# Retention and a PReLU MLP on one core: the order of all engines written out by hand

## The chip, the cores and the metric

The kernel runs on one core of a Trainium2 chip. The metric is device time in microseconds (us) of one execution, taken as the median of several; less is better. A core has TensorE (PE, whose weight loads are a row of their own, PEld), VectorE (DVE), ScalarE (ACT), GpSimd (POOL) and SyncE (SP), which here issues nearly all DMAs. Each engine works through its own instructions in order and waits on semaphores for the others.

## The reference

```python
scores = scale * np.matmul(q, k.transpose(0, 1, 3, 2))        # (8, 8, 576, 64)
gamma = 1.0 - 2.0 ** (-5.0 - np.arange(H))
Dmat = np.where(rel >= 0, gamma[:, None, None] ** rel, 0.0)    # rel = i - j
attn = np.matmul(scores * Dmat, v)
x = attn.transpose(0, 2, 1, 3).reshape(4608, 512)
h = x @ w_in                                                    # 512 -> 2048
g = np.maximum(h, 0.0) + alpha * np.minimum(h, 0.0)
out = g @ w_out                                                 # 2048 -> 512
```

Eight batches of eight heads go through a retention (attention without softmax, with a decay for each head); its result, 4608 tokens of 512, goes through two matrix products with a PReLU between them. All of it is float32.

## The kernel before

**The MLP.** Tokens come in 18 blocks `kb` of 256 (`TB`), the hidden width in eight units `u` of 256. A *cell* is one block with one unit; there are 144. PE works on rounded operands (`float32r`), so each float32 operand is split into an upper part, the exact rest and a correction, three tiles in all: ACT makes the upper part, DVE the correction, POOL the rest (`split`, L317 to 321). A cell has 24 matmuls for the first product (`mm_h`, L350, line L358) into two PSUM banks, one for each half f of the unit, tags `psh0` and `psh1`; each holds two sums of 256 columns, `ph[:, 0]` and `ph[:, 1]`. `post_h` (L364) joins the two sums of each half (ACT copy L369, DVE L370), takes the PReLU of both halves together (ACT Relu of the negative at L372 and of the positive at L373, 512 columns each, then one DVE operation for each half at L376) and splits the result into `g`. The second product (`mm_o`, L385, line L396) has 12 matmuls into four banks `po`. After the last unit of a *visit* (a block's stay with two or four units), `evacuate` (L403) joins those sums, adds what an earlier visit stored (L412) and stores `o` to DRAM (L414).

**Order of visits.** `order` (L417) first runs units 0 to 3 for all blocks and then 4 to 7; blocks 14 to 17 come in short visits in between, while the weights of units 4 to 7 are taken in. A piece of weights costs ACT L287, L288 and L311, DVE L295 to L298 and L312, POOL L300 and L314 (`piece_in`, `piece_mid`, `piece_lim`). `prepare` (L335) fetches a block's x (from the tile `xb` that the attention filled, which it also stores to DRAM, or later back from DRAM) and splits it into `lx`.

**The attention.** Batch 0 is done by the `part_` functions at the start. The other 28 pairs (a batch, two heads) are done one at a time: loads of `kx`, `qx`, `kn`, `vn` by twelve DMAs (`load_pair`, L118), scaling of q on POOL and k on ACT (`scale_pair`, L441), transposes to `kT` and `qT` on DVE (L455), and then `joint(n)` (L544). It writes pair n-1's values (`pair_values`, 32 + 4 small matmuls L526, into two banks of the tags `psh0` and `psh1`, the same as ph's), the last chunk's scores (L552), pair n's scores (L491) and chunk states (L497); starts the DMA `mt<-qT` (L501); makes the masked scores `mt` (DVE L505, ACT L512, POOL L514) and copies the values into `xb` (L536). Running sums `su` of the states (L466 to L474) go by DMA into `vn` (L480), where the next joint's values read them. `kx`, `qx`, `mt`, `kT` and `qT` have one buffer each.

**What sets the order.** The setup, batch 0 and cells 0 to 3 stand under `tc.manual_schedule()`: each engine runs them as written. `ordered.close()` and a barrier end that. In the loop over cells 4 to 143 the text only gives priorities, and the tile framework's scheduler orders each engine's instructions. On PE it keeps cells' first products going and then sets two second products behind one another, just ahead of a joint's values. `todo` says which cell has a joint after it, `later` is a list of attention work put off to the next cells, `late` says which cells take in late weights.

Of the kernel before, what the change touches and what calls it, by code (L numbers as in the profile page):

```python
# [21 lines left out]
def kernel(  # L22
# [95 lines left out]
    def load_pair(n):  # L118
        b, c = pairs[n]
        kx, qx, kn = [nat.tile([P, S], FP32, tag=t, name=f"{t[0:2]}_{n}")  # L120
                      for t in ("kx", "qx", f"kn{n % 2}")]
        kx, qx = [t.rearrange("p (n r) -> p n r", r=32) for t in (kx, qx)]
        kn = kn.rearrange("p (j d) -> p j d", d=D)
        vn = vns[n % 2]
        load_sq(kx, k, b, c)
        load_sq(qx, q, b, c)
        for t, src in ((vn, v), (kn, k)):
            for h2 in range(2):
                load_head(t[half(1 - h2), h2] if t is vn else t[half(1 - h2)], src, b, 2 * c + h2)
        return kn, kx, qx, vn  # L130
# [186 lines left out]
    def split(to, w):  # L317
        nc.scalar.mul(piece(to[0]), w, BELOW)  # L318
        nc.vector.scalar_tensor_tensor(out=piece(to[2]), in0=to[0], scalar=ONE, in1=w,  # L319
                                       op0=ALU.mult, op1=ALU.subtract)  # L320
        nc.gpsimd.tensor_tensor(out=piece(to[1]), in0=w, in1=to[0], op=ALU.subtract)  # L321
# [9 lines left out]
    xb, ready_x = {}, {}  # L331
# [3 lines left out]
    def prepare(vis):  # L335
        kb = vis["kb"]
        if vis.get("x") is not None:
            return
        if kb in xb:
            x = xb.pop(kb)  # L340
            nc.sync.dma_start(x_kept[kb], x.rearrange("p c t -> p (c t)"))
        else:
            x = ring.tile([P, NCC, TB], FP32, tag=f"x{taken[0] % 2}", name=f"xr_{taken[0]}")
            taken[0] += 1
            nc.sync.dma_start(x.rearrange("p c t -> p (c t)"), x_kept[kb])
        to = lpool.tile([P, 3, NCC, TB], FP32, tag="lx", name=f"lx_{vis['n']}")
        vis["x"] = [to[:, l] for l in range(3)]
        split(vis["x"], x)
# [14 lines left out]

    def post_h(cell):  # L364
        u = cell["u"]
        gb, gc = [mlp.tile([P, 2, TB], FP32, tag=t, name=f"{t}_{cell['n']}") for t in ("gb", "gc")]
        for f in range(2):
            ph = cell["ph"][f]
            nc.scalar.copy(gc[:, f], ph[:, 1])  # L369
            nc.vector.scalar_tensor_tensor(out=gb[:, f], in0=ph[:, 0], scalar=ONE,  # L370
                                           in1=gc[:, f], op0=ALU.mult, op1=ALU.subtract)
        nc.scalar.activation(gc, gb, ACTF.Relu, scale=-1.0)  # L372
        nc.scalar.activation(gb, gb, ACTF.Relu)  # L373
        for f in range(2):
            fc = 2 * u + f
            nc.vector.scalar_tensor_tensor(out=gb[:, f], in0=gc[:, f],  # L376
                                           scalar=nalpha[:, fc:fc + 1], in1=gb[:, f],
                                           op0=ALU.mult, op1=ALU.add)
        g = mlp.tile([P, 3, 2, TB], FP32, tag="g", name=f"g_{cell['n']}")
        cell["g"] = g  # L380
        split([g[:, l] for l in range(3)], gb)
# [3 lines left out]
    def mm_o(cell):  # L385
# [14 lines left out]
        if cell["last"]:  # L400
            evacuate(vis)

    def evacuate(vis):  # L403
        kb = vis["kb"]
        for m in range(2):
            t = mlp.tile([P, DM], FP32, tag="gc", name=f"t{m}_{vis['n']}")
            o = ring.tile([P, DM], FP32, tag=f"o{m}", name=f"o{m}_{vis['n']}")
            nc.scalar.copy(t, acc[2 * m + 1])  # L408
            nc.vector.scalar_tensor_tensor(out=o, in0=acc[2 * m], scalar=ONE, in1=t,  # L409
                                           op0=ALU.mult, op1=ALU.subtract)  # L410
            if vis["has"]:
                nc.gpsimd.tensor_tensor(out=o, in0=o, in1=vis["o"][:, m], op=ALU.add)  # L412
            t0 = kb * TB + m * P
            nc.sync.dma_start(out[t0:t0 + P, :] if vis["final"] else o_kept[kb][:, m], o)  # L414
# [9 lines left out]
    for n, (kb, us) in enumerate(order):  # L424
        vis = {"kb": kb, "n": n, "has": seen[kb] > 0}
        seen[kb] += len(us)
        vis["final"] = seen[kb] == NU
        visits.append(vis)
        for u in us:
            cells.append({"vis": vis, "u": u, "first": u == us[0], "last": u == us[-1],  # L430
                          "n": len(cells)})
# [9 lines left out]
    def scale_pair(n):  # L441
        c = pairs[n][1]
        kn, qx = loaded[n][0], loaded[n][2]
        qh = qx.rearrange("p (j x) r -> p j x r", x=2)
        nc.gpsimd.tensor_tensor(out=qh, in0=qh,
                                in1=tabx[:, None, c, :, None].to_broadcast([P, NJ, 2, 32]),
                                op=ALU.mult)
        knf = kn.rearrange("p j d -> p (j d)")
        nc.scalar.activation(knf, knf, ACTF.Copy, scale=tabk[:, c:c + 1])

    def transposes(n):
        kT = attn.tile([P, S], FP32, tag="kT", name=f"kT_{n}")
        qT = attn.tile([P, S], FP32, tag="qT", name=f"qT_{n}")
        for src, dst in ((loaded[n][1], kT), (loaded[n][2], qT)):
            nc.vector.transpose(dst, src.rearrange("p n r -> p (n r)"))  # L455
        return kT, qT
# [4 lines left out]
    def running_sums(n, even, odd):  # L461
# [5 lines left out]
        for h2 in range(2):  # L467
            nc.vector.scalar_tensor_tensor(  # L468
                out=su[half(h2), 1::2], in0=su[half(h2), 0::2], scalar=g1[half(h2)],
                in1=odd[half(1 - h2)], op0=ALU.mult, op1=ALU.add)  # L470
        for j in range(3, NJ - 1, 2):
# [4 lines left out]
        return su  # L476
# [5 lines left out]
    def pair_front(n, kT, qT, kn, vn, extra):  # L482
        c = pairs[n][1]
        mts[n] = mt = attn.tile([P, 2 * S], FP32, tag="at", name=f"mt_{n}").rearrange(
            "p (h j s) -> p h j s", h=2, s=C)
        assert C == D and NJ == 9
        ps = [ps_tile([P, 2, NM - 1, C], f"ps{p2}_{n}") for p2 in range(2)]
        for j in range(NJ - 1):
            for h2 in range(2):
# [3 lines left out]
                                 start=True, stop=True, skip_group_check=True)  # L493
        for j in range(NJ - 1):
            for h2 in range(2):
# [3 lines left out]
                                 skip_group_check=True)  # L499
        for h2 in range(2):  # L500
            nc.sync.dma_start(mt[half(h2), h2].rearrange("p j s -> p (j s)"), qT[half(h2)])  # L501
# [6 lines left out]
        for h2 in range(2):  # L508
# [8 lines left out]
        later.append(lambda: pair_sums(vn, running_sums(n, ps[0][:, 1], ps[1][:, 1])))  # L517
# [22 lines left out]
    def operands(n):  # L540
        scale_pair(n)
        turned[n] = transposes(n)

    def joint(n):  # L544
        pv = [ps_h.tile([P, 8, C], FP32, tag=f"psh{m}", name=f"pv{m}_{n}") for m in range(2)]
        extra = pv[1][:, 7]

        def last_chunk():
            if n < len(pairs):
                kT, qT = turned[n]  # L550
                for h2 in range(2):
                    nc.tensor.matmul(extra[half(1 - h2)], kT[half(h2), chunk(NJ - 1)],  # L552
                                     qT[half(h2), chunk(NJ - 1)], start=True, stop=True)

        if n - 1 in mts:
# [3 lines left out]
        if n == len(pairs):  # L559
            return  # L560
        pair_front(n, *turned.pop(n), loaded[n][0], loaded[n][3], extra)
        if n + 1 < len(pairs):
            if n + 1 not in loaded:
                loaded[n + 1] = load_pair(n + 1)
            later.append(lambda: operands(n + 1))
# [155 lines left out]
    def now(n):  # L721
        prepare(cells[n]["vis"])
        mm_h(cells[n])
# [29 lines left out]
    now(0)  # L753
# [18 lines left out]
    now(1)  # L772
# [7 lines left out]
    now(2)  # L780
# [4 lines left out]
    loaded[NPAIR] = load_pair(NPAIR)  # L785
    piece_mid(2)
    now(3)
# [8 lines left out]
    loaded[NPAIR + 1] = load_pair(NPAIR + 1)  # L796
    ordered.close()
    tc.no_sync_barrier()
# [6 lines left out]
    for b in range(2, B):  # L805
        n = NS * sum(ready[kb] == b - 1 for kb in range(2, 13)) or 6
        for i, x in enumerate({8: (0, 2, 3, 5), 12: (1, 4, 6, 9), 6: (0, 1, 3, 4)}[n]):
# [10 lines left out]
    for key in ((17, 3), (16, 2), (16, 3), (15, 2), (15, 3), (14, 2), (14, 5), (15, 4), (15, 5),  # L818
                (16, 4), (16, 5), (17, 4), (17, 5)):
        work(base[key], 2 if key in ((17, 3), (15, 3), (15, 4)) else 1)  # L820
    assert sum(late.values()) == len(pieces) // 2

    done = set()
    for cell in cells[4:]:
        n = cell["n"]
        prepare(cell["vis"])
        mm_h(cell)
        post_h(cell)
        pend.append(cell)
        if len(pend) > 2:  # L830
            mm_o(pend.pop(0))
# [4 lines left out]
        if later:  # L836
            later.pop(0)()
        for x in todo.get(n, ()):
            while later:
                later.pop(0)()  # L840
            joint(x)
            done.add(x)
        if cell["vis"]["n"] + 1 < len(visits):
            follows = visits[cell["vis"]["n"] + 1]
            kb = follows["kb"]
            if kb not in xb or NPAIR * (ready[kb] + 1) in done:
                prepare(follows)
# [6 lines left out]
        piece_lim(late.get(n, 0))  # L854
    while pend:
        mm_o(pend.pop(0))
# [28 lines left out]
```

## Time and profile before

| | |
|---|---|
| median of 3 runs (lowest to highest) | 1221.22 us (1218.66 to 1222.59) |
| the profiled execution's own time | 1220.45 us |
| its span, first to last instruction | 1218.7 us |
| PE busy | 1014.9 us, 83% |
| DVE busy | 786.8 us, 65% |
| POOL busy | 670.2 us, 55% |
| ACT busy | 608.1 us, 50% |
| mean granted TensorE clock | 0.92 |
| HBM read, written | 78.52 MB, 31.46 MB |

Busy time counts the instructions' own durations; registers, branches, semaphores and DMA issue are not in it. A row of instructions is named by its line, engine, operation and tiles (out<-in, buffer numbers left out). An arrow in a wait (`A <- B`) means that A's engine sat idle until B ended. `SPq` rows are SP issuing DMAs. The granted clock is the share of its full speed that PE was given.

### The profile page before, as it was taken

The page shows a single profiled execution, that of the slowest core. Times are in us where ns is not written, and L with a number is a line of the kernel's source. Part 1 is how long each engine was busy: PE and PEld are TensorE (multiplying, and loading weights), DVE is VectorE, ACT ScalarE, POOL GpSimd, SP SyncE. Part 2 cuts the span into 40 slices and gives each one's busy share as a digit, 9 for nine tenths or more (in the row PEclk, how much of TensorE's full clock was granted, in tenths as well). Part 3 has the DMA queues.
Part 4 walks back from the last instruction along what each step waited for, and adds up shares of the span by engine and source line. Part 5 has one row for each costly group of instructions (what it writes and reads, how often), then busy time and mean ns, then how long its engine had stood idle before and what let it go on. Part 6 is the DMA issues. An engine that isn't in the chain of part 4 may idle for free.

```text
span 1218.7 us, 22971 instructions
## 1 busy us (share of the span) xinstructions
PE 1014.9 (83%) x8813; PEld 873.0 (72%) x8813; DVE 786.8 (65%) x1306; ACT 608.1 (50%) x1219; POOL 670.2 (55%) x414
## 2 busy tenths in 40 slices
PE   5672757789788987887888876869999999999998
PEld 4562546667577766776667765758889999999996
DVE  7666646375575665473655889896776666666664
ACT  4544335455454545453555646535554555555553
POOL 6766425354354453453535667776765565665554
PEclk8775777899898999998999999989999999999999
DMA  9244366454533535554554323413232122122111
GB/s 238 89 115 121 75 133 143 103 129 112 116 107 76 133 93 136 112 139 90 124 136 158 118 92 117 138 36 123 93 131 69 62 79 70 61 79 70 48 57 52
DMA packets 250589, 127.08 MB, mean 104 GB/s; under 512 B 217952, under 2 KB 217968, under 8 KB 250480
## 3 DMA queue, kind: packets, MB, share of 16 engines
q1 hardware_dynamic: 248368, 125.08, 38.4%
q8 instruction: 69, 1.13, 0.4%
q10 hardware_dynamic: 2112, 0.53, 0.2%
q14 instruction: 40, 0.33, 0.1%
HBM read 78.52 MB, written 31.46 MB: 90 GB/s over the span
## 4 chain that ended last, share of the span: by engine, by line
PE 33%; DVE 12%; ACT 6%; issue 5%; POOL 4%; DMA 2%; SPq 0%; POOLq 0%; ACTq 0%; DVEq 0%
PE po L396 16%; PE ph L358 15%; DVE gb L376 4%; POOL g L321 2%; ACT mt L512 1%; DVE gb L370 1%; ACT g L318 1%; PE pv L526 1%; DVE o L409 1%; DVE w L312 1%; DVE wc L295 1%; DVE su L468 1%; ACT lx L318 1%; POOL wc L300 1%; ACT gb L373 1%
## 5 line engine op out<-in xcount | busy, mean ns | idle before, releaser
L396 PE MATMUL po<-w,g 128*128 128x512 f32 x1728 | 465.3, 417 | 73.7 <-POOL g L321 34.4
L358 PE MATMUL ph<-lx,w 128*128 128x256 f32 x3456 | 469.5, 293 | 59.4 <-DVE gb L370 38.2
L358 PEld LDWEIGHTS ph<-lx,w 128*128 128x128 f32 x3456 | 448.6, 199 | 83.2 <-DVE gb L370 49.1
L396 PEld LDWEIGHTS po<-w,g 128*128 128x128 f32 x1728 | 333.0, 200 | 164.5 <-POOL g L321 47.7
L321 POOL TENSOR_TENSOR g<-gb,g 128x512 fp32r<-128x512 f32 x144 | 250.3, 1738 | 267.5 <-ACT g L318 226.3
L376 DVE SCALAR_TENSOR_TENSOR gb<-gc,nalpha,gb 128x256 f32<-128x256 f32 x288 | 209.1, 766 | 78.6 <-ACT gb L373 77.6
L318 ACT ACTIVATE g<-gb 128x512 fp32r<-128x512 f32 x144 | 90.8, 631 | 198.4 <-DVE gb L376 151.5
L319 DVE SCALAR_TENSOR_TENSOR g<-g,gb 128x512 fp32r<-128x512 f32 x144 | 122.5, 851 | 68.2 <-ACT g L318 67.5
L372 ACT ACTIVATE gc<-gb 128x512 f32<-128x512 f32 x144 | 90.6, 629 | 93.0 <-DVE gb L370 93.0
L514 POOL TENSOR_TENSOR mt<-mt,mask 64x512 f32<-64x512 f32 x56 | 71.7, 1281 | 117.8 <-issue 111.2
L370 DVE SCALAR_TENSOR_TENSOR gb<-ph,gc 128x256 f32<-128x256 f32 x288 | 115.4, 417 | 28.1 <-ACT gc L369 17.7
L369 ACT COPY gc<-ph 128x256 f32<-128x256 f32 x288 | 102.4, 367 | 55.7 <-PE ph L358 53.9
L373 ACT ACTIVATE gb<-gb 128x512 f32<-128x512 f32 x144 | 91.0, 632 | 7.6
L321 POOL TENSOR_TENSOR lx<-xr,lx 128x1024 fp32r<-128x1024 f32 x24 | 80.3, 3348 | 12.8 <-ACT lx L318 12.8
L321 POOL TENSOR_TENSOR lx<-xb,lx 128x1024 fp32r<-128x1024 f32 x18 | 59.6, 3313 | 46.4 <-ACT lx L318 42.2
L536 ACT COPY xb<-pv 128x256 f32<-128x256 f32 (+3 forms) x84 | 24.0, 320 | 121.2 <-PE pv L526 108.7
L412 POOL TENSOR_TENSOR o<-o,op 128x512 f32<-128x512 f32 x48 | 65.8, 1372 | 27.1 <-DVE o L409 23.6
L526 PEld LDWEIGHTS pv<-mt,vn 128*64 128x64 f32 x1008 | 42.9, 149 | 46.6 <-DMA vn<-su 18.4
L526 PE MATMUL pv<-mt,vn 128*64 128x64 f32 x1008 | 52.5, 243 | 27.5 <-DMA vn<-su 16.7
L409 DVE SCALAR_TENSOR_TENSOR o<-po,t 128x512 f32<-128x512 f32 x84 | 57.3, 683 | 25.7 <-ACT t L408 25.4
L300 POOL TENSOR_TENSOR wc<-wc,raw 128x512 int32<-128x512 int32 x32 | 46.2, 1444 | 36.6 <-DVE wc L298 22.6
L468 DVE SCALAR_TENSOR_TENSOR su<-su,gch,ps 64x256 f32<-64x256 f32 x56 | 26.9, 480 | 55.3 <-ACT su L466 54.4
(108 smaller groups left out, 789.0 us busy)
## 6 DMA issues: line engine op xcount, KB each, us to landing
ok<-o SPq DMA_DIRECT2D x48, 256.0 KB, 2.7
xr<-xk SPq DMA_DIRECT2D x24, 512.0 KB, 3.3
op<-ok SPq DMA_DIRECT2D x24, 512.0 KB, 3.7
xk<-xb SPq DMA_DIRECT2D x18, 512.0 KB, 3.7
out_dram<-o SPq DMA_DIRECT2D x36, 256.0 KB, 2.1
raw<-in_moe_w_in_dram SPq DMA_DIRECT2D x32, 256.0 KB, 3.7
raw<-in_moe_w_out_dram SPq DMA_DIRECT2D x16, 512.0 KB, 3.4
kx<-in_k_dram SPq DMA_DIRECT2D x112, 72.0 KB, 2.6
```

The lines of the kernel that those rows point to most:

```text
L318: nc.scalar.mul(piece(to[0]), w, BELOW)
L319: nc.vector.scalar_tensor_tensor(out=piece(to[2]), in0=to[0], scalar=ONE, in1=w, op0=ALU.mult, op1=ALU.subtract)
L321: nc.gpsimd.tensor_tensor(out=piece(to[1]), in0=w, in1=to[0], op=ALU.subtract)
L358: nc.tensor.matmul(ph[:, b], piece(w_at[u, cc // 2][:, l, (cc % 2 * 2 + f) * P: (cc % 2 * 2 + f + 1) * P]), piece(x[l][:, cc]), start=(n = ...
L369: nc.scalar.copy(gc[:, f], ph[:, 1])
L370: nc.vector.scalar_tensor_tensor(out=gb[:, f], in0=ph[:, 0], scalar=ONE, in1=gc[:, f], op0=ALU.mult, op1=ALU.subtract)
L372: nc.scalar.activation(gc, gb, ACTF.Relu, scale=-1.0)
L373: nc.scalar.activation(gb, gb, ACTF.Relu)
L376: nc.vector.scalar_tensor_tensor(out=gb[:, f], in0=gc[:, f], scalar=nalpha[:, fc:fc + 1], in1=gb[:, f], op0=ALU.mult, op1=ALU.add)
L396: nc.tensor.matmul(acc[2 * m + b], piece(g[:, l, f, m * P:(m + 1) * P]), piece(w_at[u, 2 + f][:, l]), start=(cell["first"] and f == 0 and ...
L514: nc.gpsimd.tensor_tensor(out=mt[to, h2, 0:NJ - 1], in0=mt[to, h2, 0:NJ - 1], in1=mask[to, None, :].to_broadcast([C, NJ - 1, C]), op=ALU.mult)
L526: nc.tensor.matmul(pv[j >= j1][half(h2), j - (j1 if j >= j1 else 0)], vn[:, h2, j], mt[:, h2, j], start=True, stop=True)
```

## The change

- The manual schedule now goes on to the end of the kernel; the barrier is gone. Every engine runs what the loop over cells writes, in that order.
- `post_h` becomes stages, of one half of a cell where it can be: `sum_h(cell, f)`, `prelu(cell, f)`, `upper_g`, `lower_g`. The negative Relu is written back into `ph[:, 1]`, in PSUM, and DVE reads it there; half 1 of a cell followed by a joint (`short`) keeps it in SBUF. `upper_g` and `lower_g` of a cell run within the next cell.
- `mm_o` runs two cells behind `mm_h`, always between two cells' first products. `evacuate` is called for each half of a block, with other work between.
- The attention's pieces are put into `later` with a mark, "v" or "s", and popped at fixed places of a cell. A joint's scores stand ahead of the values, and its states behind the last chunk.
- `prepare` becomes `fetch_x` and `split_x` (two halves of 512 columns); `x_ahead` makes them for the next visit and fetches x back from DRAM for the visit after it.
- Loads of a pair: v, then q, k and `kn` (before: k, q, v, `kn`). Four joints of an 8-cell batch stand at cells 0, 2, 4, 6 (before 0, 2, 3, 5), of a 12-cell batch at 1, 4, 7, 10 (before 1, 4, 6, 9). Late weights come one piece a cell (before up to two).

```diff
-    def split(to, w):
+    def upper(to, w):
         nc.scalar.mul(piece(to[0]), w, BELOW)
+    def lower(to, w):
         nc.vector.scalar_tensor_tensor(out=piece(to[2]), in0=to[0], scalar=ONE, in1=w,
                                        op0=ALU.mult, op1=ALU.subtract)
         nc.gpsimd.tensor_tensor(out=piece(to[1]), in0=w, in1=to[0], op=ALU.subtract)
...
+    def sum_h(cell, f):
...
+        ph, t = cell["ph"][f], cell["t"]
+        nc.scalar.copy(t[:, f], ph[:, 1])
+        nc.vector.scalar_tensor_tensor(out=cell["g"][:, f], in0=ph[:, 0], scalar=ONE,
+                                       in1=t[:, f], op0=ALU.mult, op1=ALU.subtract)
+    def prelu(cell, f):
+        ph, g, fc = cell["ph"][f], cell["g"][:, f], 2 * cell["u"] + f
+        below = cell["t"][:, f] if f in cell.get("short", ()) else ph[:, 1]
+        nc.scalar.activation(below, g, ACTF.Relu, scale=-1.0)
+        nc.scalar.activation(g, g, ACTF.Relu)
+        nc.vector.scalar_tensor_tensor(out=g, in0=below, scalar=nalpha[:, fc:fc + 1],
+                                       in1=g, op0=ALU.mult, op1=ALU.add)
...
-        later.append(lambda: pair_sums(vn, running_sums(n, ps[0][:, 1], ps[1][:, 1])))
+        sums = running_sums(n, ps[0][:, 1], ps[1][:, 1])
+        next(sums)
+        later.append(("v", lambda: pair_sums(vn, next(sums))))
+        if n + 1 < len(pairs):
+            later.append(("v", lambda: scale_q(n + 1)))
+        later.append(("s", lambda: masked(0)))
+        later.append(("s", lambda: masked(1)))
...
+        if ps:
+            pair_scores(n, ps)
         if n - 1 in mts:
             pair_values(n - 1, loaded.pop(n - 1)[3], mts.pop(n - 1), pv, last_chunk)
...
+                load_v(n + 1)
+                load_kq(n + 1)
+            later.append(("v", lambda: transpose(n + 1, 0)))
+            later.append(("v", lambda: transpose(n + 1, 1)))
+            later.append(("s", lambda: scale_k(n + 1)))
...
-    ordered.close()
-    tc.no_sync_barrier()
...
+    def x_ahead(vis):
+        for x in visits[vis["n"] + 1:vis["n"] + 2]:
+            start_x(x)
+            if "from" in x:
+                split_x(x)
...
     for cell in cells[4:]:
...
         mm_h(cell)
-        post_h(cell)
+        before = cells[n - 1] if n > 4 else None
+        sum_h(cell, 0)
+        if before:
+            upper_g(before)
+            lower_g(before)
+        pop("v")
+        prelu(cell, 0)
+        x_ahead(vis)
+        if joints:
+            cell["short"] = (1,)
+        sum_h(cell, 1)
+        pop("v")
+        if stage_c:
+            piece_lim(1)
+        prelu(cell, 1)
         pend.append(cell)
+        second = None
         if len(pend) > 2:
-            mm_o(pend.pop(0))
+            second = pend.pop(0)
+            mm_o(second)
+            if second["last"]:
+                evacuate(second["vis"], 0)
+        x_ahead(vis)
+        pop("s")
+        if second and second["last"]:
+            evacuate(second["vis"], 1)
...
+        pop("s", 2)
+        for x in joints:
+            pop("vs", len(later))
             joint(x)
...
         piece_in(late.get(n, 0))
         piece_mid(late.get(n, 0))
-        piece_lim(late.get(n, 0))
...
+    ordered.close()
```

## The prediction

> **What bounds the kernel now.** I first cut the span into stages, by the view of busy time by stretch. Its columns are the stretch, its length, then busy us of PE, weight loads, DVE, ACT and POOL (counts in brackets), the granted PE clock, the DMA share and GB/s.
>
> ```profile
> 0.00:110.00 110.00, 60.41 (x937) 50.66 (x937) 73.42 (x133) 50.14 (x94) 69.71 (x66) 0.77 0.57 147
> 110.00:205.00 95.00, 60.16 (x685) 49.56 (x686) 55.87 (x91) 39.28 (x82) 45.34 (x29) 0.72 0.47 106
> 205.00:650.00 445.00, 375.44 (x3994) 309.89 (x3994) 253.35 (x490) 220.75 (x470) 202.68 (x126) 0.94 0.50 117
> 650.00:700.00 50.00, 40.95 (x273) 36.38 (x272) 36.86 (x55) 29.53 (x59) 29.05 (x15) 0.93 0.40 131
> 700.00:800.00 100.00, 74.33 (x414) 62.89 (x413) 90.79 (x115) 53.16 (x101) 71.24 (x42) 0.94 0.33 108
> 800.00:850.00 50.00, 42.42 (x227) 36.14 (x226) 39.72 (x55) 24.15 (x48) 36.44 (x22) 0.86 0.26 90
> 850.00:1218.00 368.00, 361.21 (x2295) 327.47 (x2293) 236.83 (x370) 191.08 (x370) 215.76 (x117) 1.00 0.22 73
> ```
>
> From 850 us on PE is busy all the time at full clock. From 700 to 800 DVE is (90.8 of 100). From 205 to 650 no engine is: PE has 70 us of holes and a clock of 0.94. Before 205 everything waits. So only the first 850 us can be won. What a cell costs when PE never waits, the chain in order of time shows, from anywhere in the last stage:
>
> ```profile
> 959.83 2.87 PE ph L358 x24
> 962.70 2.75 PE po L396 x12
> ```
>
> A cell (a block of 256 tokens with one `u`; 24 + 12 matmuls) is 5.62 us of PE. How many cells a stage holds, the ph matmuls by stretch say (busy us of PE, count in brackets):
>
> ```profile
> 205.00:650.00 445.00, 149.68 (x1130) 0.94 0.50 117
> 650.00:850.00 200.00, 86.04 (x598) 0.91 0.33 109
> ```
>
> 1130/24 = 47.1 cells in the attention stage, 9.4 us each, and 598/24 = 25 in the late-weights stage, 8.0 us each, where 5.62 would do. What PE waits for in the attention stage, the waits show (us in total, times, longest):
>
> ```profile
> PEld po L396 <- POOL g L321: 44.6, 30, 3.8
> ...
> PE po L396 <- POOL g L321: 32.9, 24, 3.5
> ```
>
> The two rows are weight loads and matmuls of one stall: the second product waits for the last operation of its own split, since the scheduler put two cells' products right behind their chain. Last, the durations of DVE's two scalar_tensor_tensor forms on 256 columns (ns min/median/max):
>
> ```profile
> L376 DVE SCALAR_TENSOR_TENSOR gb<-gc,nalpha,gb x288: 470/480/2612, 37.3 to 1207.1; 128x256 f32<-128x256 f32 x144
> L370 DVE SCALAR_TENSOR_TENSOR gb<-ph,gc x288: 385/417/426, 35.2 to 1204.8; 128x256 f32<-128x256 f32 x144
> ```
>
> L376 has both tensors in SBUF and is stretched up to 2.6 us (mean 766 ns in the groups); L370, with one of them in PSUM, never passes 426 ns.
>
> **The change, part by part.**
>
> *PReLU.* Two 512-column Relus of ACT (632 ns) become four of 256. Two of them write into the spent half of the ph bank, and the DVE operation then reads PSUM and SBUF, as L370 does. DVE: 288 operations at 417 instead of 766 ns, less 28 in joint cells that keep SBUF: 260 x 0.349 = 91 us less. The trace has no DVE operation just like it: ends 385 and 766 ns; I take 417, the same form. ACT: no Relu into PSUM is shown either; ends are 316 ns (half of 632) and 632; I take 372, the 256-column copy of L369. Then ACT's cell grows from 2x0.37 + 3x0.63 = 2.62 to 6x0.37 + 0.63 = 2.85 us, which 5.62 us of PE hides. The DVE gain counts only where DVE is the bound.
>
> [...]
>
> *Split a cell later, second product two cells behind.* g is made in the next cell's gaps and read one more cell later, so the stall on POOL's split goes. What is late next: the ph bank, now held until the PReLU's DVE operation and no longer only the sum. In a plain cell its chain from the end of f0's matmuls is copy 0.37, upper 0.63, two Relus 0.74 on ACT, then DVE 0.42: 2.2 us, with the split's 0.69 of DVE inside it; PE is back at the bank 4.2 us after. Free.
>
> *Attention in the gaps (cells with a joint).* PE per pair is 2.7 us (below, from pv at 433.22 to the next ph at 435.55, and 0.34 for four pv before). With a joint every second cell PE alone needs 11.24 + 2.7 = 13.9 us a pair. I walk the engines through it, in us after the joint cell's first matmul, row durations. DVE: sum 1.9-2.3, split 2.6-3.3, kT 0.74 to 4.0, PReLU to 4.5, sum to 4.9, qT 0.77 to 5.7: the scores stand at 5.62, on time. pv ends at 7.6, the copies to xb at 8.4, the su copy at 8.9, two sums of 0.48 at 9.9. Second cell: sum, split and four su operations (0.41 each) bring its first PReLU to 13.9, when PE wants that bank. Then ACT has the four masked copies (4 x 0.469 = 1.9) from 15.1 to 17.0, ahead of the next cell's copy, which is ready at 15.4: 1.6 us late, and with a block's two evacuations (0.58 each) between them 2.7. Half a split of x on DVE adds 0.7 in one cell of four. So I charge 2.4 us a joint; the ends are 0.5, if ACT's copies find other holes, and 6.6 (below).
>
> *SP's order.* All of a pair's loads now stand behind mt<-qT, which waits for pv, and vn<-su behind the loads. The timeline of before has every piece:
>
> ```profile
> 433.22 1.20 PE L526 MATMUL pv<-mt,vn 128*64 128x64 f32 x32
> ...
> 434.45 1.11 SPq L501 DMA_DIRECT2D mt<-qT  x2
> ...
> 435.65 2.98 SPq L107 DMA_DIRECT2D kx<-in_k_dram  x4
> ...
> 438.67 1.58 SPq L107 DMA_DIRECT2D qx<-in_q_dram  x3
> ...
> 440.30 1.34 SPq L112 DMA_DIRECT2D vn<-in_v_dram  x2
> ...
> 441.68 1.32 SPq L112 DMA_DIRECT2D kn<-in_k_dram  x2
> ...
> 443.78 1.45 SPq L480 DMA_DIRECT2D vn<-su  x2
> ```
>
> New order from the end of pv: mt 1.1, v 1.3, q 2.3, k 3.0, kn 1.3, su 1.3, landing 3.3 (the stage's median), pv 1.2: 14.8 us round. That is under 13.9 + 2.4 = 16.3, so the queue does not set the pace, with 1.5 us to spare. kx is there after 1.1 + 1.3 + 2.3 + 3.0 + 2.6 = 10.3; DVE comes to it at about 11.3.
>
> *Sum of the attention stage.* 47 x 5.62 + 22 joints x 2.7 + 22 x 2.4 = 264 + 59 + 53 = 376, and 10 for the clock: 386 instead of 445, **-59**. The clock: PE's own work here would be 264 + 59 = 323 at the last stage's pace, 375 are recorded, so some 50 us go to the 0.94 clock and stretched matmuls; with half the holes I keep 10. [...]
>
> *Late weights.* DVE's 49 L376 here take 43 us; at 417 ns 20, so 23 less. 700-800: 90.8 - 9.6 = 81 of DVE at the same occupancy, 89 us. 650-700: 7.4 cells of PE, 42, say 45. 800-850: DVE 32, POOL's 36 stays, say 42. Together 176 of 200: **-24**. Pieces are one a cell now, POOL's 71 of 100 hides below DVE. If the PSUM form cost 766 ns, these 24 would be 0 and 0.7 a joint would be added: +40.
>
> *Before 205.* To cell 3 the order is the same but for loads (q ahead of k); I give 0. Pairs 4 to 10 stand 16.5 us apart (states at 103.6 and 202.8, six intervals); the loop of 14.8 gives 6 x 1.7, **-10**. The barrier between the stages goes too, inside this.
>
> *After 850.* PE-bound before and after: 0. x a visit ahead moves loads of 3.3 us that lie under PE already.
>
> 1220.45 (profiled execution, span 1218.7) - 59 - 24 - 10 = **1127**. The median shown, 1221.22, is 0.8 above that execution; nothing hangs on it.
>
> **Rivals.**
>
> *The gaps hold everything*: 0.5 us a joint and 5 for the clock give 264 + 59 + 11 + 5 = 339 (-106), late weights 160 (-40), -15 early: **1060**. For it: in a pair's 13.9 us ACT has 2 x 2.85 + 1.1 (half a block's x and evacuation) + 3.9 (masked 1.88, kn 0.77, su 0.37, xb 0.9) = 10.7 of work, and DVE about as much. Against: ACT's masked copies stand ahead of the next cell's copy.
>
> *The pair loop stays as long as it is* (DMA share up, the xk stores between): 18.2 us a pair instead of 16.3 takes 42 of the 59 back, the 10 go too: 1127 + 42 + 10 = **1180**. For it: DMA busy half of this stage already.
>
> *Written order blocks*, the slower side. DVE has the kT transpose ahead of the cell's PReLU. If kx lands late, DVE stops, the ph bank stays held, and PE, which runs nothing out of order, stops too. From 2.4 + 93/22 = 6.6 us a joint the change loses. Waits on loads of up to 5.5 (qx) and 8.0 (kn) are in the whole waits list, so 9 a joint is thinkable: 1127 + 22 x 6.6 = **1272**. Against: 1.0 us to spare, landings of 2.6.
>
> *It moves and gives nothing*: gains of late weights, spent in joints: 1220.
>
> **Numbers.** Forecast 0.50 (own range 1090 to 1160), all in the gaps 0.22, loop 0.14, nothing 0.05, blocked 0.09. Faster 0.50 + 0.22 + 0.14 = 0.86, within 0.3% (about what a measurement here can tell from no change) 0.05, slower 0.09. The range takes in the two neighbours, 1050 to 1195.
>
> **What would show it.** Right: the PReLU row on DVE near 417 ns with a maximum under 500; no wait of po on POOL's split; 5.6 us a cell from 850 us before the change's end on; pv every 16 us. Wrong: DVE waiting for DMA kx or qx, PE waiting for the ph bank by more than 3 us a joint, or PE waiting for vn<-su.

## The result, and the profile after

The changed kernel is **slower**: 1255.76 us (median of 4, 1251.33 to 1262.4) against 1220.37 for the kernel before on the same chip, a ratio of 1.029 (95% interval 1.024 to 1.035). The forecast was 1127, with a range to 1195. The profiled execution is the longest of the four, 1262.4 us, with a span of 1260.7, so stage figures below run some 7 us above the median.

The busy time by stretch, with the columns of before (length, then PE, weight loads, DVE, ACT, POOL, granted clock, DMA share, GB/s):

```profile
110.00:205.00 95.00, 39.71 (x524) 35.09 (x524) 44.46 (x77) 33.40 (x74) 34.18 (x25) 0.66 0.35 77
205.00:650.00 445.00, 363.95 (x3723) 316.08 (x3721) 288.28 (x474) 224.47 (x541) 179.66 (x132) 0.87 0.48 112
...
700.00:800.00 100.00, 87.39 (x558) 77.78 (x557) 76.27 (x120) 63.85 (x148) 63.55 (x40) 0.97 0.33 114
```

From 110 to 205 PE does 40 us of work where it did 60, at a clock of 0.66. In the attention stage PE issues 3723 matmuls in 445 us where it issued 3994; it is busy nearly as long (364 against 375 us), because the clock fell from 0.94 to 0.87. DVE, which was to be relieved, is busier (288 against 253 us). Only the late-weights stage moves the way that was forecast (PE is busy for 87 of the 100 us from 700 on, before 74).

Since stages shift, stretches of equal time hold different cells. A better ruler is the start of each cell's first product: every cell has 24 ph matmuls, so it is the start of every 24th one. Before, cell 10 starts at 208 us, cell 60 at 675 and cell 84 at 867, and the first product of the last cell (143) ends at 1204. The table has what each version loses (+) or wins (-) against these in each stage, in us, each in its profiled execution:

| stage | forecast | changed kernel | best version (below) |
|---|---|---|---|
| to cell 10 | -10 | +27 | +1 |
| cells 10 to 60, attention | -59 | +27 | -62 |
| cells 60 to 84, late weights | -24 | -12 | -12 |
| cell 84 to the end of the last first product | 0 | -1 | -1 |

So 37 us of the miss are early, 86 in the attention stage and 12 in the late weights. What PE waits for in the attention stage (us in total, times, longest):

```profile
PE ps L511 <- DVE qT L478: 53.7, 16, 4.6
PE ph L372 <- DVE ga L392: 20.5, 13, 2.9
```

The wait for POOL's split is gone, as forecast. In its place PE waits for `qT`: the scores now stand on PE ahead of everything else of a joint, and DVE makes `qT` too late. It also waits 20.5 us for the ph bank, which the PReLU (L392) holds. The operations that keep DVE, in the attention stage (busy us, mean ns, idle before; the last row is kT's transpose, which is not kept waiting):

```profile
L324 DVE SCALAR_TENSOR_TENSOR g<-g,ga 128x512 fp32r<-128x512 f32 x44 | 68.2, 1551 | 3.9 <-ACT g L321 3.1
L496 DVE SCALAR_TENSOR_TENSOR su<-su,gch 128x64 f32<-128x64 f32 x63 | 45.5, 722 | 1.5
...
L478 DVE STREAM_TRANSPOSE kT<-kx 128x576 f32<-128x576 f32 x20 | 15.3, 766 | 0.1
```

The same two in the same stretch of the kernel before:

```profile
L319 DVE SCALAR_TENSOR_TENSOR g<-g,gb 128x512 fp32r<-128x512 f32 x47 | 46.3, 986 | 18.7 <-ACT g L318 18.0
...
L472 DVE SCALAR_TENSOR_TENSOR su<-su,gch 128x64 f32<-128x64 f32 x66 | 26.1, 395 | 1.6
```

The split's operation takes 1551 ns here (986 before, median over the whole kernel 693) and a running sum 722 (395 before, median 285). Both read two tensors from SBUF. What POOL does at the moment when they start decides it: of the 44 splits, the 20 that start while POOL is idle take 692 ns in the mean, and the 18 that start within one of POOL's mask multiplies take 2602. The PReLU and the sum, which read one of theirs from PSUM, are not stretched; the same line of the PReLU with both in SBUF (the `short` halves) is, up to 1559 ns (ns min/median/max):

```profile
L392 DVE SCALAR_TENSOR_TENSOR ga<-ph,nalpha,ga x260: 434/483/485, 36.4 to 1248.9; 128x256 f32<-128x256 f32 x130
L392 DVE SCALAR_TENSOR_TENSOR ga<-gt,nalpha,ga x28: 483/484/1559, 118.0 to 705.2; 128x256 f32<-128x256 f32 x28
...
L384 DVE SCALAR_TENSOR_TENSOR ga<-ph,gt x288: 384/415/426, 35.0 to 1247.6; 128x256 f32<-128x256 f32 x144
```

How this delays a joint, DVE's timeline shows (start us, us). It is the second cell of a pair of cells:

```profile
522.42 0.42 DVE L384 SCALAR_TENSOR_TENSOR ga<-ph,gt 128x256 f32<-128x256 f32 x1 [1.96 <-POOL mt L546]
523.00 2.50 DVE L324 SCALAR_TENSOR_TENSOR g<-g,ga 128x512 fp32r<-128x512 f32 x1 [0.16 <-ACT g L321]
525.43 0.77 DVE L478 STREAM_TRANSPOSE kT<-kx 128x576 f32<-128x576 f32 x1
526.12 0.44 DVE L392 SCALAR_TENSOR_TENSOR ga<-ph,nalpha,ga 128x256 f32<-128x256 f32 x1
526.49 0.40 DVE L384 SCALAR_TENSOR_TENSOR ga<-ph,gt 128x256 f32<-128x256 f32 x1
526.82 0.76 DVE L478 STREAM_TRANSPOSE qT<-qx 128x576 f32<-128x576 f32 x1
```

And POOL's in the same moment:

```profile
521.05 2.65 POOL L546 TENSOR_TENSOR mt<-mt,mask 64x512 f32<-64x512 f32 x2 [1.67 <-issue]
523.67 1.28 POOL L326 TENSOR_TENSOR g<-ga,g 128x512 fp32r<-128x512 f32 x1
```

The split is issued at 523.00, while POOL multiplies masks, and ends at 525.50, half a microsecond after POOL's own part of the split has ended at 524.95. It needs 0.69. (The sum before it, at 522.42, starts when ACT's copy for it ends at 522.31, behind four masked copies, as the walk had it.) In the written order kT, the first PReLU, the sum and qT all stand behind it. PE waits for qT:

```profile
527.72 1.24 PE L511 MATMUL ps<-qT,kT 64*64 64x64 f32 x32 [2.76 <-DVE qT L478]
528.89 2.19 PE L565 MATMUL pv<-mt,vn 128*64 128x64 f32 x36
```

The scores start after 2.76 us of an idle PE, and run at half rate (32 matmuls in 1.24 us), and so do the values (36 in 2.19 us); in joints of run 4 below that had not waited these took 0.69 and 1.27. From one joint's last chunk to the next, 511.06 to 531.0, are 20 us; between 205 and 700 us there are 17 such distances with two cells in them, and their mean is 20.6. The walk gave 16.3.

In these rows the forms with two tensors in SBUF were stretched beside POOL's work (the split here 2.50 us, against 0.69 beside an idle POOL), and those with one were not (maxima of 426 and 485 ns). How POOL's work holds them up is not shown.

The early loss has another face. From ACT's timeline, in cell 4:

```profile
115.43 0.63 ACT L321 ACTIVATE lx<-xr 128x512 fp32r<-128x512 f32 x1 [8.65 <-DMA xr<-xk]
115.96 0.35 ACT L383 COPY gt<-ph 128x256 f32<-128x256 f32 x1
```

Half of the next visit's x is split in the middle of the cell (`x_ahead`), ahead of the cell's own second copy. Its load was issued only at 111.40, behind twelve loads of a pair. ACT waits 8.65 us for it, the copy waits behind, the ph bank stays held and PE waits 10.3 us.

### The profile page after: what moved, and what is told of

Same layout as the page of the kernel before. It is cut to its first block, busy times and chain, and to the rows that moved or that the text cites. A ratio compares the mean times of both kernels' runs of the same rounds, so it can differ in the third digit from the quotient of the medians.

```text
span 1260.7 us, 23249 instructions
## 1 busy us (share of the span) xinstructions
PE 1016.1 (81%) x8813; PEld 895.9 (71%) x8813; DVE 816.3 (65%) x1348; ACT 659.1 (52%) x1549; POOL 648.4 (51%) x456
## 4 chain that ended last, share of the span: by engine, by line
PE 43%; DVE 20%; ACT 7%; issue 6%; DMA 3%; SPq 1%; POOL 1%; DVEq 0%; POOLq 0%; ACTq 0%
PE ph L372 20%; PE po L424 16%; PE pv L565 4%; DVE su L496 3%; DVE lx L324 2%; DMA vn<-su 2%; DVE g L324 2%; DVE ga L392 2%; ACT mt L544 2%; DVE ga L384 2%; PE ps L511 2%; DVE wc L298 2%; ACT g L321 1%; PE ps L520 1%; DVE kT L478 1%
## 5 line engine op out<-in xcount | busy, mean ns | idle before, releaser
L326 POOL TENSOR_TENSOR g<-ga,g 128x512 fp32r<-128x512 f32 x144 | 238.4, 1655 | 309.0 <-ACT g L321 279.6
L390 ACT ACTIVATE ph<-ga 128x256 f32<-128x256 f32 x260 | 100.9, 388 | 202.5 <-DVE ga L384 200.3
L384 DVE SCALAR_TENSOR_TENSOR ga<-ph,gt 128x256 f32<-128x256 f32 x288 | 120.0, 417 | 127.6 <-ACT gt L383 104.1
L392 DVE SCALAR_TENSOR_TENSOR ga<-ph,nalpha,ga 128x256 f32<-128x256 f32 x260 | 124.0, 477 | 103.8 <-ACT ga L391 103.6
L383 ACT COPY gt<-ph 128x256 f32<-128x256 f32 x288 | 104.6, 363 | 137.0 <-PE ph L372 136.5
L324 DVE SCALAR_TENSOR_TENSOR g<-g,ga 128x512 fp32r<-128x512 f32 x144 | 168.5, 1170 | 11.4 <-ACT g L321 7.0
L391 ACT ACTIVATE ga<-ga 128x256 f32<-128x256 f32 x288 | 120.3, 418 | 17.3
L326 POOL TENSOR_TENSOR lx<-xr,lx 128x512 fp32r<-128x512 f32 x48 | 84.1, 1752 | 23.2 <-ACT lx L321 22.5
L326 POOL TENSOR_TENSOR lx<-xb,lx 128x512 fp32r<-128x512 f32 x36 | 54.7, 1523 | 78.2 <-ACT lx L321 75.0
L321 ACT ACTIVATE g<-ga 128x512 fp32r<-128x512 f32 x144 | 91.5, 636 | 3.4 <-DVE ga L392 2.2
L434 DVE SCALAR_TENSOR_TENSOR o<-po,t 128x512 f32<-128x512 f32 x84 | 57.0, 689 | 16.3 <-ACT t L433 15.0
```

The lines of the kernel that those rows point to most:

```text
L383: nc.scalar.copy(t[:, f], ph[:, 1])
L384: nc.vector.scalar_tensor_tensor(out=cell["g"][:, f], in0=ph[:, 0], scalar=ONE, in1=t[:, f], op0=ALU.mult, op1=ALU.subtract)
L390: nc.scalar.activation(below, g, ACTF.Relu, scale=-1.0)
L391: nc.scalar.activation(g, g, ACTF.Relu)
L392: nc.vector.scalar_tensor_tensor(out=g, in0=below, scalar=nalpha[:, fc:fc + 1], in1=g, op0=ALU.mult, op1=ALU.add)
```

## The experiments

Two theories at first. **T1, queue and lock** (the expectations' name for it): DVE's operations with two SBUF inputs take longer beside POOL's work (a split that starts within a mask multiply 2602 ns against 692), and in the written order PReLU and transposes queue behind them. **T2, held bank**: the ph bank, now held until the PReLU, stops PE (the mechanism of the slower rival). All changes are shown against the changed kernel unless said otherwise. For each run: the median, the ratio to the kernel before with its interval, and the cells' starts against it (the changed kernel has cell 10 at +27, cell 60 at +55 and cell 84 at +43). The kernel of run 7 is also called version 7, that of run 9 version 9.

**1. The scheduler again** for cells 4 to 143, with the new pieces.

```diff
     load_kq(NPAIR + 1)
+    ordered.close()
+    tc.no_sync_barrier()
     in_flight[0] = 0
```

> The changed kernel with its new pieces, but the scheduler orders cells 4 to 143 again (the manual schedule ends where it ended before, barrier included). Theory 1 (queue and lock): in the written order DVE's operations with two SBUF inputs stand behind POOL's operations and block the PReLU and the transposes queued after them, and PE then misses the scores and loses its clock. The order is the cause, so the scheduler brings it back to 1190 to 1220 us. Theory 2 (held bank): the new pieces are the cause, above all the ph bank that is held until the PReLU's last operation; then it stays at 1240 or above, whoever orders.

1245.94, 1.021 (1.018 to 1.023); cell 10 at +5, cell 60 at +30. The early loss goes with the written order, the attention's loss does not: it is lost with the scheduler too, with PE's scores never late there (at most 2.3 us) and all but one joint at full rate. There DVE's split of x is the stretched operation, 2468 ns: 11 of its 22 in this stage start within a mask multiply of POOL and take 4080 ns in the mean, and 9 that start while POOL is idle take 688. So "the order alone" is refuted; the new pieces and their places in the text lose under either, and the same hold sits on another operation. From cell 10 to cell 60 PE is busy 412 us here (393 before) and idle 80 (74 before), so most of the loss lies in slower matmuls; how it comes about in this version is not shown.

**2. The PReLU alone**, in the kernel before.

```diff
-        nc.scalar.activation(gc, gb, ACTF.Relu, scale=-1.0)
-        nc.scalar.activation(gb, gb, ACTF.Relu)
...
+        for f in range(2):
+            fc, below = 2 * u + f, cell["ph"][f][:, 1]
+            nc.scalar.activation(below, gb[:, f], ACTF.Relu, scale=-1.0)
+            nc.scalar.activation(gb[:, f], gb[:, f], ACTF.Relu)
+            nc.vector.scalar_tensor_tensor(out=gb[:, f], in0=below, ...)
```

> The kernel before with one part of the change alone: the PReLU by halves, the negative Relu written into the spent half of the ph bank. Theory 1: the PReLU's operation on DVE falls from 766 to about 480 ns, the late-weights stage gains some 20 us, the attention stage loses nothing: 1190 to 1210. Theory 2: the bank is held until the PReLU, PE waits for it in the attention stage: 1230 or more.

1192.2, 0.977 (0.975 to 0.979): 28 us faster. This part of the change is good, and T2 as the cause of the loss is refuted. The held bank is not free: in the attention stage PE waits 24.4 us for it (`PE ph L358 <- DVE gb L376`, 14 times), but only 19 us for the operands of the second product, where it waited 55. Of 26 us at cell 84, 5 are won before cell 10, 15 in the attention stage and 6 in the late weights, where I had put all of it.

**3. The split of the previous cell behind both PReLU halves** (`upper_g`, `lower_g` moved from between `sum_h` and `pop("v")`).

```diff
         sum_h(cell, 0)
-        if before:
-            upper_g(before)
-            lower_g(before)
         pop("v")
...
         prelu(cell, 1)
+        if before:
+            upper_g(before)
+            lower_g(before)
         pend.append(cell)
```

> The changed kernel, with the split of the cell before (ACT upper, DVE and POOL lower) moved behind both PReLU halves, so that PReLU and transposes no longer queue behind an operation that POOL can block. Theory 1: in a joint's cell the scores come about 2.5 us earlier and PE's clock does not drop after the stall: 22 joints x 2 to 4 us less, 1165 to 1210. Theory 2: the bank is still held until the PReLU, only the split's own 0.7 us goes: 1235 to 1255.

1232.74, 1.011 (1.007 to 1.014), outside the ranges of both theories; cell 60 at -2 (changed kernel +55), but cell 84 at +1 and the end at +11. From cell 10 to cell 60, 54 us are won, and the late weights and the last cells give back 26 of it, where the second product now waits 7 us for POOL's part of the split. The rest of that loss is not traced; run 7 keeps the old place in those cells and doesn't have it. In the attention stage POOL's masks are all there, and yet the split and a running sum are hardly stretched (755 and 281 ns; in the changed kernel those that start while POOL is idle take 692 and 283):

```profile
L324 DVE SCALAR_TENSOR_TENSOR g<-g,ga 128x512 fp32r<-128x512 f32 x49 | 37.0, 755 | 1.7
...
L496 DVE SCALAR_TENSOR_TENSOR su<-su,gch 128x64 f32<-128x64 f32 x72 | 20.3, 281 | 1.7
```

**4. POOL's mask multiplies left out**, so that scores of later positions stay in; one execution, and so no interval.

```diff
-            nc.gpsimd.tensor_tensor(
-                out=mt[to, h2, 0:NJ - 1], in0=mt[to, h2, 0:NJ - 1],
-                in1=mask[to, None, :].to_broadcast([C, NJ - 1, C]), op=ALU.mult)
```

> The changed kernel without the causal mask of the whole chunks' scores (POOL's two multiplications of 1.28 us a pair are left out, so the diagonal blocks stay unmasked); nothing else moves. Theory 1: the split's DVE operation is no longer locked out by them, its mean falls from 1170 to under 1000 ns, and the joint's cell gets 1.5 to 3.5 us shorter: 1175 to 1220. Theory 2: POOL has nothing to do with it, 1245 to 1260.

1201.62 us, 54 less than the changed kernel, the order untouched. The split in the attention stage:

```profile
L324 DVE SCALAR_TENSOR_TENSOR g<-g,ga 128x512 fp32r<-128x512 f32 x49 | 39.3, 802 | 4.3 <-ACT g L321 3.3
```

1551 has become 802 ns. It was POOL's masks that stretched it. The running sums stay at 659 ns; they stand beside POOL's part of the split, which is still there (19 of 72 start within it and take 1314 ns in the mean). Cell 60 is at -5.

**5 and 6. The early order.** In the fifth run the next visit's x is fetched a cell earlier, and k's scaling and the transposes (with the masked scores that stand before them in `later`) go ahead of the weight pieces of cells 4 and 5; in the sixth the fetch alone.

```diff
+    fetch_x(visits[2])
     operands(NPAIR)
...
         if n in (4, 5):
+            pop("vs", len(later))
             piece_in(2)
```

> The changed kernel with two things moved ahead in cells 4 and 5: the load of the next visit's x is issued a cell earlier, and the k scaling and the transposes stand ahead of the four weight pieces. Theory E (the 25 us lost by cell 10 are queue order: a joint cell's copy behind half an x split on ACT that waits for its load, 8.65 us, and the transposes behind weight pieces, 12 us): 1256 - 15 to -22 = 1234 to 1241, cell 10 back to within 10 us of the kernel before. Rival (the early pairs are slow because their loads come late, whatever stands ahead): 1250 or more, and the waits move onto kx or kn.

> The changed kernel with one of the two early edits alone: the load of the next visit's x a cell earlier. Theory E: it takes away ScalarE's wait of 8.65 us at the x load, and leaves the transposes behind the weight pieces: 1256 - 8 = 1248, 1243 to 1252, cell 6 back at the time of the kernel before and cell 8 still some 15 us late. Rival (the two stand in one chain and either edit alone gives nothing or all): 1255 or more, or 1240 or less.

Both: 1237.8, 1.014 (1.012 to 1.016), cell 10 at +12. The fetch alone: 1241.41, 1.016 (1.012 to 1.020), just under its range, cell 6 at +1, cell 8 at +10 and cell 10 at +17. The load is the larger part, some 14 us against 8 expected, and the transposes the smaller, some 4 against 12, within the overlap of the two intervals: my split of the two was off, their sum was not.

**7. Early order, and the split behind in cells 5 to 57 only** (as runs 3 and 5, with `n <= 57`).

("The same" in it is run 5.)

> The same, and the split of the previous cell moved behind both PReLU halves, but only in cells 5 to 57 (with the move in all cells, 53 us were won by cell 60 and 10 to 20 lost after it). Theory Q (queue order in the attention stage is one cause, the early order another, and they add): 1256 - 20 - 53 = 1183, 1175 to 1200. Rival (both moves free the same wait, another one such as the loads then sets the pair's pace): 1215 or more.

1187.63, 0.973 (0.971 to 0.974), cell 10 at +6, cell 60 at -20. The two causes add. PE still waits 47.5 us for qT, but now because DVE waits for a DMA (kT's row: idle before it, and what ended it):

```profile
L478 DVE STREAM_TRANSPOSE kT<-kx 128x576 f32<-128x576 f32 x22 | 17.1, 778 | 48.9 <-DMA vn<-su 35.0 <-DMA ok<-o 13.9
```

In the changed kernel that idle time was 0.1 us, in run 3 it is 47.1 us already. What kT waits for is not kx. The sums `su` and `kT` are tiles of one tag, `kT`, and so share one buffer: the transpose can't write it before the transfer vn<-su has read the sums out of it. In all 22 joints of the stage kT starts within 0.3 us of that transfer's landing, in the mean 3.1 us after the last of kx's loads has landed. In SP's queue the transfer stands behind the loads of v, q and k, and is issued 9.3 us (mean) after mt<-qT.

**8 and 9. The mask on VectorE** from PSUM, with one SBUF tensor, in place of ACT's copies and POOL's multiplies: in the changed kernel, and in version 7.

```diff
-                nc.scalar.activation(mt[to, h2, p2:NJ - 1:2], ps[p2][x, 0], ACTF.Copy,
-                                     scale=pf[x, 1, h:h + 1])
-            nc.gpsimd.tensor_tensor(...)
+                nc.vector.scalar_tensor_tensor(
+                    out=mt[to, h2, p2:NJ - 1:2], in0=ps[p2][x, 0], scalar=pf[x, 1, h:h + 1],
+                    in1=mask[x, None, :].to_broadcast([C, NM - 1, C]),
+                    op0=ALU.mult, op1=ALU.mult)
```

> The changed kernel with the mask multiplied on VectorE straight from PSUM (four operations of 64 by 256 columns, one SBUF tensor each) in place of ScalarE's four scaled copies and GpSimd's two multiplies. Theory L (lock: the operations with two SBUF inputs are held off by GpSimd's masks): without the masks 54 us were won; the four DVE operations add 4 x 0.42 = 1.7 us a joint, 37 in 22 joints at most, some of it in gaps: 1205 to 1235, split near 0.8 us in the attention stage. Rival C (without the masks it was the shorter chain to pv and less ScalarE work that won, DVE's own load is what delays the transposes): 1250 or more, split still over 1.3 us.

> All three edits at once. Theory Q with L: the early 20 are won in full; the moved split and the absent masks free the same DVE queue, so they overlap: 1165 to 1195. Rival C (DVE has no room for the masks): slower than the version with GpSimd's masks, 1200 or more.

1208.06, 0.989 (0.986 to 0.992), cell 60 at +3: with the masks multiplied the hold on the split is gone, and although DVE has four more operations of 483 ns a joint, 48 us are won:

```profile
L324 DVE SCALAR_TENSOR_TENSOR g<-g,ga 128x512 fp32r<-128x512 f32 x48 | 37.4, 779 | 1.0
```

In version 7 the same edit gives 1186.81 (0.972, 0.970 to 0.974) against 1187.63, nothing: there the split took 793 ns already.

**10 to 12. The q and k loads ahead of `mt<-qT`**: in version 7, in version 9, and in the changed kernel.

```diff
+        had = list(loaded)
+        if n + 1 < len(pairs) and n + 1 not in loaded:
+            load_kq(n + 1)
         pair_front(n, ps, extra)
         if n + 1 < len(pairs):
-            if n + 1 not in loaded:
+            if n + 1 not in had:
                 load_v(n + 1)
-                load_kq(n + 1)
```

> The version with the early order mended and the split moved behind in cells 5 to 57, and in it a pair's q and k loads issued ahead of mt<-qT instead of behind it and the v load. There PE still waits 47 us for qT in the attention stage, DVE comes free and waits for kx (kT: 48.9 us idle), and SP waits 150 us at mt<-qT for pv and qT. Theory S (with the queue on DVE mended, SP's loop of 18.3 us a pair sets the pace): the loads start 2 to 3 us earlier in each of 22 joints, 1188 - 40 = 1148, 1135 to 1165, kT no longer waits for a load. Rival (PE and DVE work fill the pair's time): 1178 or more.

> The same with the mask on VectorE. While the loads set the pace, that was worth nothing (1186.8 against 1187.6). Theory S: with the loads ahead DVE's room matters, and the two versions part by more than 5 us; since DVE has 299 of 445 us here against 254, I expect this one to be the slower, 1145 to 1175. Rival: equal within 3 us.

> The changed kernel with only the q and k loads put ahead of mt<-qT. Theory Q (in the changed kernel DVE's own queue delays the transposes; its kT operation is never kept by a load there, 0.1 us idle): 1248 to 1262, no gain. Rival (SP's loop set the pace in the changed kernel too): 1225 or less.

(Theory S takes kT's wait for one for kx; the starts under run 7 show that it is one for the sums' transfer.)

In version 7: **1145.48, 0.939 (0.936 to 0.941)**, the best of all, 75 us faster than the kernel before. kT's idle time falls:

```profile
L478 DVE STREAM_TRANSPOSE kT<-kx 128x576 f32<-128x576 f32 x22 | 17.1, 776 | 17.3 <-DMA vn<-su 17.2
```

With q's and k's loads out of its way, vn<-su is issued 3.1 us after mt<-qT and not 9.3, and kT starts 9.3 to 14.2 us after the end of pv, where it was 12.0 to 14.5; 17 of its 22 starts still follow the landing of vn<-su within 0.4 us. So, as far as these starts show, the edit pays by the place of that transfer in SP's queue. A buffer of its own for `su`, or its transfer ahead of the loads, which would isolate it, was not run.

With the mask on VectorE it is 1149.46, 0.942 (0.940 to 0.945): the direction was as expected, but 4 us, between the over 5 of the theory and the 3 of its rival and with overlapping intervals, don't tell the two versions apart. In the changed kernel the same edit gives 1250.67, 1.025 (1.023 to 1.028), 5 us less, an interval that overlaps the changed kernel's: no transfer can be the limit while DVE comes to kT late (kT idle 0.0 us).

**13. Idle matmuls ahead of the scores**, to part the stall from the clock.

```diff
         if ps:
+            for _ in range(16):
+                nc.tensor.matmul(ps[0][:, 0], piece(w_at[now[0]["u"], 0][:, 0, 0:P]),
+                                 piece(now[0]["vis"]["x"][0][:, 0]), start=True, stop=True, ...)
             pair_scores(n, ps)
```

> The changed kernel with 16 idle matmuls of 128 by 256 (some 1.9 us, on operands that are already there, into columns that the scores then overwrite) ahead of each joint's scores. They fill part of the wait for qT and shorten no other engine's work. Theory H (about half of the attention stage's loss is the clock: after waits of 2.8 us and more 15 of 24 joints have their scores at half rate, 1.24 instead of 0.69 us, and PE is busy 8.12 us a cell against 7.61 without the masks, 0.5 x 47 = 24 us): 1225 to 1240, at most 5 joints at half rate. Rival (the wait itself is all, the filler only takes PE's time): 1250 to 1275.

1234.21, 1.011 (1.009 to 1.014): 21 us faster by work that is thrown away. The stretch of the attention stage:

```profile
205.00:650.00 445.00, 387.64 (x4188) 341.96 (x4188) 300.12 (x496) 234.48 (x564) 190.70 (x140) 0.96 0.50 117
```

The clock is 0.96 instead of 0.87, though some 350 of these 4188 matmuls are the idle ones (16 in each of some 22 joints). Read off PE's timeline between 195 and 700 us, the scores ran at half rate (over 1.0 us) in 15 of 24 joints of the changed kernel, in 5 of 24 here, in 7 of 24 with the split behind, in 4 of 24 without masks and in 4 of 23 of the best version. In the kernel before it was 1 of 23.

## Why the prediction was wrong, by its steps

**"Attention in the gaps" failed.** The walk priced DVE's split at 0.69 us and the sums at 0.41, as if nothing stood beside them. I had read the stretched maxima in L376 and used them for the PReLU's gain only; L319 and L472 in the same groups (986 and 395 ns in this stage) read two SBUF tensors as well. The walk then placed them in the same moments as POOL's masks and split. Measured: 20.6 us from joint to joint in place of 16.3, so 6.7 us a joint over PE's own 13.9 and not 2.4. Runs 4 and 8 show that the masks were needed for it, run 3 that the place in DVE's queue was: each of these edits brings back 51 to 60 us by cell 60.

**The clock was priced too low.** The 10 us for it were my estimate, from 323 and 375 us of PE's work and half the holes gone; instead the granted clock of the attention stage fell from 0.94 to 0.87. Half-rate scores followed waits of 1.9 to 13.1 us in the changed kernel, most of them of 2.8 to 4.6, and waits of 2.8 to 3.3 were followed by full rate in five joints. Run 13 puts some 20 us on this. PE's busy time agrees: from cell 10 to cell 60 it is 403 us in the changed kernel and 373 in run 4, and its idle time 91 and 64, so about half of what the masks cost is slower matmuls behind the waits and not the waits themselves. Why the same wait is followed by half rate in one joint and by full rate in another, no run here shows.

**"The queue does not set the pace, with 1.5 us to spare"** was right for the changed kernel (run 12) and wrong as soon as DVE was mended, and not by kx. The walk let kT start when kx has landed, 10.3 us after the end of pv, and overlooked that `kT` has its buffer from `su`. In the walk's own terms vn<-su lands at 1.1 + 1.3 + 2.3 + 3.0 + 1.3 + 1.3 + 3.3 = 13.6 us, and in version 7 kT starts 12.0 to 14.5 us after the end of pv. 42 us hung on the queue (version 7 against 10).

**"Before 205: the same, -10"** failed: +27. The -10 rested on a miscount: from 103.6 to 202.8 us there are six pairs' states and so five intervals, of 37.3, 13.6, 17.3, 14.7 and 16.2 us. The last four have a mean of 15.5, so a loop of 14.8 had some 3 us to win there and not 10. The changed kernel's first states come at 117.4, 14 us later, and the sixth at 227.7, 25 later. I had counted the moved loads of q and k and not that `x_ahead` makes ACT wait for an x load that is issued just before. I counted what a moved step issues on SP, and not what the engine that then waits has behind it.

**PReLU**: mechanism right, size off. 477 ns mean against 417 forecast and 766 before; maximum 485, as said. **Late weights**: -12 instead of -24, the forecast having put the PReLU's whole gain there (run 2 alone has -6 there). **Held bank free**: not as the change stands, 20.5 us of waits in the attention stage; in version 7, where the split stands behind the PReLU, 5.6 are left, which fits the walk's chain of 2.2 us on a DVE that isn't held. **After 850**: right.

**The rivals.** The one that came true is "written order blocks", at a price (6.7 us a joint) at its turning point of 6.6, and with the early loss added. Its queue was right, kT ahead of the PReLU on DVE; its cause was not: no transfer was late (kT idle 0.1 us), an operation of DVE itself was. I gave it 0.09 because I looked for the blocking only among DMAs. The forecast's own attention stage is what the best version reaches (-62 for -59, 16.3 us between joints two cells apart), with three edits that the change didn't have. That the figures meet is in part luck: the walk had neither the lowered clock nor the wait for the sums' transfer in it.

## What to carry to other kernels

When an engine's order is written by hand, price each operation by its stretched mean in the stage it goes to and by what the neighbouring engine runs in the same moment, since all that stands behind it pays the difference. Put the work that another engine waits for (here transposes and PReLU) ahead of work that only the next cell needs, and loads ahead of a DMA that waits for a late result, so that what stands behind both is issued sooner (here vn<-su 3.1 us after mt<-qT and not 9.3). Look for tiles that share a buffer, since the second waits for the first one's transfer (kT 35.0 us in version 7), and read which DMA ended a wait before putting it down to the operand's load. Small waits of PE (here of 1.9 to 4.6 us) can be followed by a lowered clock (0.87 in the attention stage, and 0.96 with idle matmuls in the wait), and its busy share hides that (364 us against 375 before): compare matmuls done (3723 against 3994).

## What the runs showed of the hardware that I had not expected

- A DVE scalar_tensor_tensor over 256 columns takes 417 ns with a constant as scalar (L384) and 477 to 483 with a scalar for each partition (L392, L544), whether its other input is in PSUM or not (L376 of before: median 480, all in SBUF). The 63 ns between the medians of L376 and L370 in the kernel before (480 and 417), from which I took 417 for the form that reads PSUM, follow the scalar in every row here. The arithmetic differs between these rows too, but with a constant over 512 columns the split (multiply and subtract, L324) and L315 (multiply and add) have minima of 678 and 677 ns.
- ACT's Relu over 256 columns takes 388 ns into PSUM (L390) and 418 into SBUF (L391).
- Sixteen matmuls thrown away before each joint made the kernel 21 us faster.
